# Attention and mixture of experts in one kernel on one Trainium2 core: the last small chunk alone ahead of its pair, three weight units converted ahead, local products in halves

## The chip, the cores and the metric

The kernel runs on one core of one Trainium2 chip, in one launch. The metric is the device time of that launch in microseconds (us). Lower is better.

## What is computed

The reference does two things one after the other. Attention takes q, k, v of 4 batches, 8 heads, 576 tokens and 64 values per head:

```python
q_d = q.reshape(B, H, Sd, factor, D).mean(axis=3)      # factor 4; the same for k and v
out_d = sm_attn(q_d, k_d, v_d)                         # softmax attention over 144 mean tokens
out_up = np.repeat(out_d, factor, axis=2)
mask = np.abs(pos[:, None] - pos[None, :]) < factor    # local: 7 keys for each token
attn = softmax(where(mask, scale * q @ k.T, -1e9))
x = (out_up + attn @ v)                                # as 2304 tokens x 512 values
```

The second part mixes 8 experts over these tokens. The gate P comes from `x @ w_gate` by 8 rounds of normalising rows and columns over all 2304 tokens, so no expert's output can be weighted before all of x is known:

```python
for e in range(E):                                     # 8 experts, D = 512, F = 1024
    h = np.maximum(x @ w1[e], 0.0)
    out += P[:, e:e + 1] * (h @ w2[e])
```

## The kernel before, in words

**Chunks and units.** The 576 mean tokens of the four batches lie behind each other and are cut into six chunks: three small ones (0, 1 and 5, 64 mean tokens, which are 256 tokens) and three large ones (2, 3, 4, 128 mean tokens, 512 tokens). The experts' work is cut into units. A unit is one expert and one eighth of its hidden values for one piece, a piece being a small chunk alone, a pair of small chunks, or a large chunk. `order` (L1001 to L1004) is the list of pieces and experts, eight units each: chunk 0 alone with 4 experts (units 0 to 31, counted from 0), the pair (0, 1) with the other 4 (32 to 63), chunk 2 with 8 (64 to 127), then the pair (1, 5) with 4 and chunk 5 alone with 4 (128 to 191). Chunks 3 and 4 come last in another form (L1401 on, seven products in place of eight).

**One unit on the engines.** `mm1` (L952) multiplies x by a 512 x 128 block of w1 into `psh`, 12 matmuls; ScalarE writes `hh`, the relu rounded to fp32r, and VectorE writes `hl`, what the rounding lost (L970). `mm2` (L975) multiplies these by w2 into `psy`, 3 matmuls for each 128 tokens. TensorE's order is mm1 of unit n+1, then mm2 of unit n, so `hl` of a unit is wanted one mm1 after it can be made. Each raw weight tile `r` becomes a high part (`w1h`, `w2h`, ScalarE, L196) and a low part (`w1l`, `w2l`, GpSimd at L203 or VectorE at L206) in `w_convert` (L185). Three units of raw tiles are held, and four converted units.

**Local attention.** `l_gen` (L268) works through nine local units (one for a small chunk, two for a large one). For each of four heads VectorE multiplies queries by a window of keys (`prod`, L277) and sums (L300); softmax; then it multiplies values by weights (L339) and sums into `lo` (L370). `x_gen` (L757) transposes `lo` on TensorE (`psx`), adds the mean attention (`xs`, L783) and splits x into high (L792) and low (L796 GpSimd, L799 VectorE). Mean attention itself is `d_gen`, fed by sums on GpSimd (`p_gen`, L424: L449 and L453).

**What sets the order.** Instructions of each engine run in the order in which the program writes them. That order is set by a planner with its own clocks (`clk`) and costs: `dma` (L154) for transfers, `pump` (L934) which lets the local thread go ahead between an mm1 and its `hl` as long as the planned VectorE time is 2.5 us short of the planned `hh`. A loop in the first phase (L1130) steps all threads until x of the next piece is there, before it writes the next mm1. When the gate is known the first phase ends at the next full group of eight units; results until then are spilled to DRAM (L1150) and read back (`back_load`, L1207) by the second phase.

In `w_convert` the name `l2` is an argument and later a tile, so that the test on it is always true for the second weight, and GpSimd makes every `w2l`:

```python
    def w_convert(*deps, need=1e9, l2=None):
        ...
        l2 = pl.tile([128, DM], F32R, tag="w2l", name="w2l")
        ...
            if l2 != nc.vector if r is r2 and l2 is not None else t_pool <= max(need, t_dve + 1):
```

Of the kernel before, what the change touches and what calls it, by code (L numbers as in the profile page):

```python
# [20 lines left out]
def attention_moe_kernel(  # L21
# [10 lines left out]
    nc = tc.nc  # L32
    B, H, S, D = q.shape
    NT, DM = out.shape
    E = moe_w_gate.shape[1]
# [118 lines left out]
    def dma(kb, *deps):  # L154

        return at("dma", 0.05 + kb * 0.375, *deps) + 2.0
# [28 lines left out]
    def w_convert(*deps, need=1e9, l2=None):  # L185
# [9 lines left out]
        for r, h, l in ((r1, h1, l1), (r2, h2, l2)):  # L195
            nc.scalar.activation(out=h, in_=r, func=AF.Copy)  # L196
            t = act(512, t_raw, *deps)
            t_pool = max(clk["pool"], t) + 1.3
            if r is r2 and can("p", clk["pool"]):
                t_pool += 1  # L200
            t_dve = max(clk["dve"], t) + 0.6
            if l2 != nc.vector if r is r2 and l2 is not None else t_pool <= max(need, t_dve + 1):
                nc.gpsimd.tensor_tensor(out=l, in0=r, in1=h.bitcast(F32), op=ALU.subtract)  # L203
                done = max(done, pool(512, t))
            else:
                nc.vector.tensor_tensor(out=l, in0=r, in1=h.bitcast(F32), op=ALU.subtract)  # L206
                done = max(done, dve(512, t))
# [60 lines left out]
    def l_gen():  # L268

        for u in range(len(lunits)):  # L270
# [17 lines left out]
            nr = R  # L288
# [4 lines left out]
            for h in range(4):  # L293
                pr, t = ahead[h] if h in ahead else (prod_tile(ap1), 0.0)
                for r0 in range(0, R, nr):
# [7 lines left out]
                    dve(nr * W * D, t)  # L303
            if u + 1 < len(lunits):
                l_load_win(u + 1, k, l_k)
                l_load_q(u + 1)
# [69 lines left out]
            if u + 1 < len(lunits):  # L376
                l_load_win(u + 1, v, l_v)
# [574 lines left out]
    def mm1(piece, n):  # L952
# [16 lines left out]
        pump(t, t_h - 2.5)  # L969
        nc.vector.scalar_tensor_tensor(  # L970
# [21 lines left out]
    with tc.manual_schedule():  # L992
# [11 lines left out]
        order += [((1, NC - 1), e) for e in range(n_small)] + [((NC - 1,), e) for e in range(n_small, E)]  # L1004
# [78 lines left out]
        while not x_ok(0):  # L1083
# [15 lines left out]
            if n_cv[0] < 4 and v_done and max(w_raw[n_cv[0]][2], clk["act"], clk["pool"] - 1.0) <= r:  # L1099
                w_convert()  # L1100
                continue
            th[nm].step()
        while n_cv[0] < 4:
            w_convert(need=0.0)
        started[0] = True
# [17 lines left out]
        while True:  # L1123
# [6 lines left out]
            while n_cv[0] < 4:  # L1130
                w_convert(need=0.0)
# [199 lines left out]
        for si, (piece, e, f, n) in enumerate(steps):  # L1331
# [9 lines left out]
            while n_cv[0] < min(n + 5, len(units)):  # L1341
                w_convert(t2, l2=nc.vector if len(piece) == 1 else nc.gpsimd)
# [3 lines left out]
            if si >= 4:  # L1346
# [4 lines left out]
                next(tg, None)  # L1351
# [206 lines left out]
```

## Time and profile before

| what | value |
|---|---|
| runs | 1683.18, 1675.39, 1684.88 us (median 1683.18) |
| profiled execution, own time | 1685.94 us |
| its span | 1684.2 us |
| TensorE busy | 1645.5 us, 98% of the span |
| VectorE, ScalarE, GpSimd busy | 959.1, 642.5, 997.4 us |
| HBM | 125 GB/s over the span |

The span is the time from the first to the last instruction in the profile. TensorE's matmuls are pipelined: one of 512 columns is shown with 0.39 us, but the next one starts 0.227 us later. So its work is read from starts, and its losses from idle time and from the granted clock. "psy L982 <- DVE hl L970" reads: the matmul of line 982, which writes `psy`, waited for VectorE's instruction of line 970, which writes `hl`.

### The profile page before, as it was taken

To read this page: it belongs to the slowest core of one execution; us is meant where nothing else is said; L and a number is where in the kernel's file an instruction comes from. 1 tells how busy PE (TensorE), PEld (TensorE's weight loads), DVE (VectorE), ACT (ScalarE), POOL (GpSimd) and SP (SyncE) were. 2 spreads that over 40 slices of the span, in tenths; PEclk is the share of its full clock that TensorE was granted. 3 is DMA by queue.
4 is the path that set the end of the run, shared out by engine and by line. 5 is a ranking of instruction groups with operands and counts; after the bars stand their busy time and mean duration, and the time that the engine had idled before them with its cause. 6 is when DMAs were issued, how large, how long until landed. Compare 5 with 4: busy or idle time off the path is not lost.

```text
span 1684.2 us, 22138 instructions
## 1 busy us (share of the span) xinstructions
PE 1645.5 (98%) x7941; PEld 1357.0 (81%) x7941; DVE 959.1 (57%) x1130; ACT 642.5 (38%) x1306; POOL 997.4 (59%) x803
## 2 busy tenths in 40 slices
PE   6899899999999999999999999999999999999999
PEld 5788788788788877887888898888888888888887
DVE  7567896788779677343865324444444444444444
ACT  1554354444444443333333554333333333333332
POOL 5678787669669465444545897554444445444441
PEclk9999999999999999999999999999999999999999
DMA  8877677567577653344665762111111111111111
GB/s 192 188 220 192 167 196 194 160 171 175 170 172 185 155 143 118 107 120 137 197 209 187 229 186 87 53 55 56 51 50 50 51 51 51 53 54 56 50 38 50
DMA packets 220623, 211.70 MB, mean 126 GB/s; under 512 B 12898, under 2 KB 161904, under 8 KB 220514
## 3 DMA queue, kind: packets, MB, share of 16 engines
q1 hardware_dynamic: 211298, 193.51, 42.4%
q10 hardware_dynamic: 9216, 16.78, 2.7%
q8 instruction: 62, 1.02, 0.3%
q14 instruction: 47, 0.39, 0.1%
HBM read 190.85 MB, written 19.40 MB: 125 GB/s over the span
## 4 chain that ended last, share of the span: by engine, by line
PE 86%; POOL 5%; DMA 4%; DVE 3%; issue 2%; ACT 1%; SPq 0%; POOLq 0%; ACTq 0%; DVEq 0%
PE psh L961 22%; PE psm L1401 18%; PE psy L980 7%; PE psy L982 7%; PE psy L981 7%; PE psy L1474 7%; PE psy L1472 7%; PE psy L1473 7%; POOL w2l L203 2%; POOL w1l L203 2%; DMA r<-in_moe_w_dram 1%; DVE lo L370 1%; DMA lq<-in_q_dram 1%; DMA dr<-in_v_dram 1%; PE pss L674 1%
## 5 line engine op out<-in xcount | busy, mean ns | idle before, releaser
L203 POOL TENSOR_TENSOR w1l<-r,w1h 128x512 fp32r<-128x512 f32 x191 | 264.5, 1385 | 233.8 <-ACT w1h L196 205.8
L203 POOL TENSOR_TENSOR w2l<-r,w2h 128x512 fp32r<-128x512 f32 x192 | 289.7, 1509 | 73.0 <-ACT w2h L196 72.8
L980 PE MATMUL psy<-w2h,hh 128*128 128x512 f32 x640 | 255.6, 399 | 3.6 <-ACT hh L967 3.6
L982 PE MATMUL psy<-w2h,hl 128*128 128x512 f32 x640 | 250.8, 392 | 7.7 <-DVE hl L970 6.4
L970 DVE SCALAR_TENSOR_TENSOR hl<-psh,hh 128x512 fp32r<-128x512 f32 (+1 forms) x192 | 114.9, 599 | 244.0 <-ACT hh L967 243.5
L981 PE MATMUL psy<-w2l,hh 128*128 128x512 f32 x640 | 250.6, 392 | 0.0
L1319 POOL TENSOR_TENSOR w2l<-r,w2h 128x512 fp32r<-128x512 f32 x64 | 83.2, 1300 | 281.3 <-ACT w2h L1318 281.3
L1195 DVE SCALAR_TENSOR_TENSOR acc<-psy,lg,acc 128x512 f32<-128x512 f32 x140 | 103.9, 750 | 199.9 <-PE psy L1474 198.7
L967 ACT ACTIVATE hh<-psh 128x512 fp32r<-128x512 f32 (+1 forms) x192 | 100.7, 525 | 300.3 <-PE psh L961 297.8
L196 ACT ACTIVATE w2h<-r 128x512 fp32r<-128x512 f32 x192 | 120.9, 630 | 195.7 <-POOL w1l L203 103.3
L961 PE MATMUL psh<-xhs,w1h 128*128 128x256 f32 (+1 forms) x512 | 177.4, 346 | 0.6 <-ACT xhs L792 0.6
L961 PE MATMUL psh<-xls,w1h 128*128 128x256 f32 (+1 forms) x512 | 174.9, 342 | 0.5 <-POOL xls L796 0.4
L961 PE MATMUL psh<-xhs,w1l 128*128 128x256 f32 (+1 forms) x512 | 174.5, 341 | 0.0
L1285 POOL TENSOR_TENSOR c1l<-r,c1h 128x512 fp32r<-128x512 f32 (+1 forms) x128 | 145.0, 1159 | 33.9 <-ACT c1h L1282 33.9
L982 PEld LDWEIGHTS psy<-w2h,hl 128*128 128x128 f32 x640 | 120.5, 188 | 35.9 <-DVE hl L970 8.3
L980 PEld LDWEIGHTS psy<-w2h,hh 128*128 128x128 f32 x640 | 121.0, 189 | 26.2 <-ACT hh L967 3.8
L981 PEld LDWEIGHTS psy<-w2l,hh 128*128 128x128 f32 x640 | 121.0, 189 | 21.7
L1282 ACT ACTIVATE c1h<-r 128x512 fp32r<-128x512 f32 (+1 forms) x128 | 65.0, 567 | 176.0 <-POOL r L1290 176.0
L196 ACT ACTIVATE w1h<-r 128x512 fp32r<-128x512 f32 x192 | 120.0, 625 | 25.0 <-DMA r<-in_moe_w_dram 15.4
L370 DVE TENSOR_REDUCE lo<-prod 128x256 f32<-128x1792 f32 x36 | 123.5, 3433 | 8.3 <-PE psx L774 8.1
L961 PEld LDWEIGHTS psh<-xhs,w1h 128*128 128x128 f32 x512 | 98.8, 193 | 13.9 <-ACT xhs L792 1.4
L961 PEld LDWEIGHTS psh<-xls,w1h 128*128 128x128 f32 x512 | 99.1, 194 | 13.1 <-POOL xls L796 0.7
(183 smaller groups left out, 3568.4 us busy)
## 6 DMA issues: line engine op xcount, KB each, us to landing
r<-in_moe_w_dram SPq DMA_DIRECT2D x512, 256.0 KB
spill<-sp ACTq DMA_DIRECT2D x56, 256.0 KB
s<-spill SPq DMA_DIRECT2D x56, 256.0 KB
dr<-in_k_dram SPq DMA_DIRECT2D x32, 144.0 KB
dr<-in_v_dram SPq DMA_DIRECT2D x32, 144.0 KB
dr<-in_q_dram SPq DMA_DIRECT2D x24, 144.0 KB
lw<-in_v_dram SPq DMA_DIRECT2D x4, 640.0 KB
lw<-in_k_dram SPq DMA_DIRECT2D x2, 1120.0 KB
```

What stands on the lines that cost most here:

```text
L196: nc.scalar.activation(out=h, in_=r, func=AF.Copy)
L203: nc.gpsimd.tensor_tensor(out=l, in0=r, in1=h.bitcast(F32), op=ALU.subtract)
L370: nc.vector.tensor_reduce(out=ot[:, r0:r0 + nr, h % 2], in_=pr[:, r0:r0 + nr].rearrange("p r w d -> p r d w"), axis=AX.X, op=ALU.add,)
L961: nc.tensor.matmul(out=ps, lhsT=w[:, kk], rhs=x[:, kk], start=(i == 0), stop=(i == len(seq) - 1))
L980: nc.tensor.matmul(out=y, lhsT=hh[:, ts], rhs=h2, start=(f == 0), stop=False)
L981: nc.tensor.matmul(out=y, lhsT=hh[:, ts], rhs=l2, start=False, stop=False)
L982: nc.tensor.matmul(out=y, lhsT=hl[:, ts], rhs=h2, start=False, stop=(f == NF - 1))
L1285: nc.gpsimd.tensor_tensor(out=ls[i][:, s], in0=r[:, s], in1=hs[i][:, s].bitcast(F32), op=ALU.subtract)
L1401: nc.tensor.matmul(out=ps, lhsT=wt[:, kk], rhs=xt[:, kk], start=start and j == 0, stop=j == len(seq) - 1, skip_group_check=not start,)
L1472: nc.tensor.matmul(out=y, lhsT=hh[:, f, ts], rhs=h2, start=(f == 0), stop=False)
L1473: nc.tensor.matmul(out=y, lhsT=hh[:, f, ts], rhs=l2, start=False, stop=False)
L1474: nc.tensor.matmul(out=y, lhsT=hl[:, f, ts], rhs=h2, start=False, stop=(f == 3))
```

## The change

Six edits, most of them to the planner. (1) The planner's cost of a transfer goes from 0.375 to 0.55 us per unit of size. (2) `w_convert` gets an argument `low2` of its own name; VectorE makes `w2l` for units of a chunk alone in the second phase. (3) Local products and sums are issued in halves of two tokens of the four, from local unit 1 on; the load of the value window of local unit 1 moves from the end of local unit 0 to a place inside local unit 1. (4) Three units are converted before the first mm1, not four, and the planner's clocks are set to their maximum there; after each of the first two mm1 the local thread is stepped until 1.5 us of VectorE time have passed. (5) Chunk 5 alone comes ahead of the pair (1, 5). (6) Spilled tiles are read back during the pair alone, and the preparation of the last phase takes one step per unit.

```diff
-        return at("dma", 0.05 + kb * 0.375, *deps) + 2.0
+        return at("dma", 0.05 + kb * 0.55, *deps) + 2.0
-    def w_convert(*deps, need=1e9, l2=None):
+    def w_convert(*deps, need=1e9, low2=nc.gpsimd):
-            if l2 != nc.vector if r is r2 and l2 is not None else t_pool <= max(need, t_dve + 1):
+            if low2 is nc.gpsimd if r is r2 else t_pool <= max(need, t_dve + 1):
...
-            nr = R
+            nr = R if u == 0 else R // 2
...
+                if u == 1 and h == 0:
+
+                    l_load_win(1, v, l_v)
...
-            if u + 1 < len(lunits):
+            if 0 < u < len(lunits) - 1:
                 l_load_win(u + 1, v, l_v)
...
         pump(t, t_h - 2.5)
+        if n < 2:
+
+            was = clk["dve"]
+            while clk["dve"] < was + 1.5:
+                th["l"].step()
...
-        order += [((1, NC - 1), e) for e in range(n_small)] + [((NC - 1,), e) for e in range(n_small, E)]
+        order += [((NC - 1,), e) for e in range(n_small, E)] + [((1, NC - 1), e) for e in range(n_small)]
...
-            if n_cv[0] < 4 and v_done and max(w_raw[n_cv[0]][2], clk["act"], clk["pool"] - 1.0) <= r:
+            if n_cv[0] < 3 and (v_done or n_cv[0] < 2) and max(w_raw[n_cv[0]][2], clk["act"], clk["pool"] - 1.0) <= r:
...
-        while n_cv[0] < 4:
+        while n_cv[0] < 3:
             w_convert(need=0.0)
+        now = max(clk["dve"], clk["act"], clk["pool"])
+        clk["pe"] = clk["dve"] = clk["act"] = now
...
-            while n_cv[0] < 4:
-                w_convert(need=0.0)
...
-                w_convert(t2, l2=nc.vector if len(piece) == 1 else nc.gpsimd)
+
+                alone = len(steps[n_cv[0] - n_a][0]) == 1
+                w_convert(t2, low2=nc.vector if alone else nc.gpsimd)
...
-            if si >= 4:
+            if len(piece) == 2:
+
                 for _ in range(2):
                     back_load()
                     back_load()
                     back_add()
-                next(tg, None)
+            if si >= 4:
                 next(tg, None)
```

Because a planner writes the order, the diff doesn't tell where instructions end up. Three places matter. In the changed kernel lines are numbered up to 11 higher from L304 on.

ScalarE at the start, where x of chunk 0 is made (`xhs`) and the first two units begin (`hh`). The raw tile of the fourth unit is r_419 before and r_413 in the change. Before:

```order
L196 ACTIVATE w1h<-r_173 128x512
L196 ACTIVATE w2h<-r_174 128x512
L792 ACTIVATE xhs<-xs 128x256 x4
L196 ACTIVATE w1h<-r_419 128x512
L196 ACTIVATE w2h<-r_420 128x512
L967 ACTIVATE hh<-psh 128x256 x2
L819 ACTIVATE gs<-psg 16x256
```

and now:

```order
L196 ACTIVATE w1h<-r_173 128x512
L196 ACTIVATE w2h<-r_174 128x512
L603 ACTIVATE od<-pso 128x2x64 x2
L795 ACTIVATE xhs<-xs 128x256 x4
L970 ACTIVATE hh<-psh 128x256 x2
L822 ACTIVATE gs<-psg 16x256
L196 ACTIVATE w1h<-r_413 128x512
L196 ACTIVATE w2h<-r_414 128x512
```

The fourth unit's conversion now stands behind the two `hh`, where it stood ahead of them.

VectorE at the last local unit (chunk 5), the value products and sums up to the last `xs`. Before, in units 108 to 114:

```order
L339 TENSOR_TENSOR prod<-lw,sc 128x1792
L970 SCALAR_TENSOR_TENSOR hl<-psh,hh 128x512
L370 TENSOR_REDUCE lo<-prod 128x4x64
L339 TENSOR_TENSOR prod<-lw,sc 128x1792
L970 SCALAR_TENSOR_TENSOR hl<-psh,hh 128x512
L370 TENSOR_REDUCE lo<-prod 128x4x64
L339 TENSOR_TENSOR prod<-lw,sc 128x1792
L970 SCALAR_TENSOR_TENSOR hl<-psh,hh 128x512
L783 TENSOR_TENSOR xs<-psx,od 128x256
```

and now, from `hl` of unit 127 (first row here) to `hl` of units 128 to 130 (last row); the first rows and the last:

```order
L978 SCALAR_TENSOR_TENSOR hl<-psh,hh 128x512
L342 TENSOR_TENSOR prod<-lw,sc 128x896
L373 TENSOR_REDUCE lo<-prod 128x2x64
L342 TENSOR_TENSOR prod<-lw,sc 128x896
L373 TENSOR_REDUCE lo<-prod 128x2x64
...
L342 TENSOR_TENSOR prod<-lw,sc 128x896
L373 TENSOR_REDUCE lo<-prod 128x2x64
L786 TENSOR_TENSOR xs<-psx,od 128x256 x2
L978 SCALAR_TENSOR_TENSOR hl<-psh,hh 128x256 x3
```

Between those two `hl` there stand 6 products, 6 sums and 4 `xs`; before, no two `hl` of this stretch have more than one product and one sum between them, and the last `xs` of chunk 5 stands ahead of `hl` of unit 114.

TensorE at the same place of the change: the end of mm2 of unit 126, the transposes of chunk 5's `lo`, and mm1 of unit 128.

```order
L990 MATMUL psy<-w2h,hl 128x512
L777 MATMUL psx<-ident,lo 128x64 x16
L964 MATMUL psh<-xhs,w1h 128x256
L964 MATMUL psh<-xls,w1h 128x256
L964 MATMUL psh<-xhs,w1l 128x256
```

mm2 of unit 127 stands behind this mm1. Before, these transposes stand at units 111 and 114, and the first phase ends at unit 128; now it ends at unit 152, with 62 spilled tiles in place of 56.

## Rows read from the trace of the kernel before

**Rows 1.** The page's part 1, busy time of each engine.

```profile
PE 1645.5 (98%) x7941; PEld 1357.0 (81%) x7941; DVE 959.1 (57%) x1130; ACT 642.5 (38%) x1306; POOL 997.4 (59%) x803
```

**Rows 2.** Busy time by stretch: from:to, length, then busy us (and instructions) of PE, PEld, DVE, ACT, POOL, the granted clock, DMA share, GB/s.

```profile
0.00:60.00 60.00, 42.29 (x288) 32.20 (x288) 38.66 (x52) 13.99 (x41) 32.28 (x24) 1.00 0.94 197
60.00:180.00 120.00, 106.46 (x708) 92.68 (x709) 86.79 (x85) 60.62 (x145) 98.04 (x71) 0.94 0.70 196
180.00:760.00 580.00, 578.08 (x2748) 470.47 (x2747) 420.14 (x411) 251.32 (x545) 384.33 (x268) 1.00 0.59 159
760.00:1050.00 290.00, 288.32 (x1444) 244.26 (x1444) 138.70 (x187) 118.12 (x217) 185.92 (x146) 1.00 0.58 178
1050.00:1684.00 634.00, 630.37 (x2758) 517.43 (x2756) 274.84 (x397) 198.44 (x358) 296.82 (x295) 1.00 0.17 51
```

**Rows 3.** TensorE's timeline (start, us, instruction, in brackets the idle time before it and what ended it): the end of mm1 of unit 1 and mm2 of unit 0, the four later waits of the first 180 us, and two rows of an undisturbed unit, 11 matmuls apart.

```profile
57.17 0.28 PE L961 MATMUL psh<-xhs,w1h 128*128 128x256 f32 x1
...
58.48 0.28 PE L961 MATMUL psh<-xhs,w1l 128*128 128x256 f32 x1
62.35 0.50 PE L980 MATMUL psy<-w2h,hh 128*128 128x512 f32 x1 [3.58 <-ACT hh L967]
...
112.18 0.50 PE L982 MATMUL psy<-w2h,hl 128*128 128x512 f32 x1 [1.26 <-DVE st L692]
...
118.78 0.48 PE L705 MATMUL pst<-ident,pp 80*72 80x80 f32 x2 [2.41 <-ACT pp L685]
...
151.41 0.43 PE L774 MATMUL psx<-ident,lo 64*128 64x64 f32 x4 [2.14 <-DVE lo L370]
...
176.19 0.59 PE L982 MATMUL psy<-w2h,hl 128*128 128x512 f32 x1 [4.79 <-DVE hl L970]
...
191.09 0.39 PE L980 MATMUL psy<-w2h,hh 128*128 128x512 f32 x1
...
193.58 0.39 PE L982 MATMUL psy<-w2h,hl 128*128 128x512 f32 x1
```

**Rows 4.** ScalarE's timeline at the start.

```profile
60.70 0.63 ACT L196 ACTIVATE w1h<-r 128x512 fp32r<-128x512 f32 x1 [7.09 <-DMA r<-in_moe_w_dram]
...
61.93 0.64 ACT L967 ACTIVATE hh<-psh 128x256 fp32r<-128x256 f32 x2
```

**Rows 5.** The clock: stretches of 3.4 us that follow the waits which ended at 62.35, 118.78, 151.41 and 176.19 us, with the columns of rows 2.

```profile
63.80:67.20 3.40, 3.40 (x16) 3.09 (x15) 2.15 (x2) 1.19 (x3) 3.40 (x3) 0.50 0.52 153
118.40:121.80 3.40, 3.02 (x15) 3.02 (x16) 2.65 (x4) 2.54 (x7) 1.58 (x3) 0.50 0.83 260
152.60:156.00 3.40, 3.40 (x15) 2.85 (x14) 1.09 (x3) 1.21 (x3) 0.68 (x2) 0.50 0.94 160
176.50:179.90 3.40, 3.40 (x9) 2.65 (x8) 3.40 (x3) 0.00 (x0) 1.16 (x2) 0.50 0.22 74
```

**Rows 6.** GpSimd and VectorE at the same times: GpSimd's start after the first wait; a VectorE product at 166.08 us with the `hl` behind it, and GpSimd's instructions meanwhile; then `hl` of unit 31.

```profile
61.41 1.27 POOL L203 TENSOR_TENSOR w1l<-r,w1h 128x512 fp32r<-128x512 f32 x1 [7.10 <-DMA r<-in_moe_w_dram]
...
166.08 9.71 DVE L277 TENSOR_TENSOR prod<-lq,lw 128x1792 f32<-128x1792 f32 x1
175.72 0.41 DVE L970 SCALAR_TENSOR_TENSOR hl<-psh,hh 128x256 fp32r<-128x256 f32 x1
...
166.43 1.29 POOL L203 TENSOR_TENSOR w1l<-r,w1h 128x512 fp32r<-128x512 f32 x1
...
172.64 1.27 POOL L203 TENSOR_TENSOR w2l<-r,w2h 128x512 fp32r<-128x512 f32 x1
173.86 3.06 POOL L449 TENSOR_TENSOR dr<-dr 72x512 f32<-72x512 f32 x1
...
102.80 1.27 POOL L449 TENSOR_TENSOR dr<-dr 72x512 f32<-72x512 f32 x1
...
177.01 0.73 POOL L453 TENSOR_TENSOR dq<-dr 72x256 f32<-72x256 f32 x1
...
177.98 0.41 DVE L970 SCALAR_TENSOR_TENSOR hl<-psh,hh 128x256 fp32r<-128x256 f32 x1
178.31 2.01 DVE L277 TENSOR_TENSOR prod<-lq,lw 128x1792 f32<-128x1792 f32 x1
```

**Rows 7.** Groups of instructions by line and shape: busy us, mean ns of one, idle before and its releasers. The row of xl has 512 elements and two SBUF operands.

```profile
L370 DVE TENSOR_REDUCE lo<-prod 128x256 f32<-128x1792 f32 x36 | 123.5, 3433 | 8.3 <-PE psx L774 8.1
...
L277 DVE TENSOR_TENSOR prod<-lq,lw 128x1792 f32<-128x1792 f32 x34 | 94.2, 2772 | 3.6 <-DMA lw<-in_k_dram 3.0
...
L970 DVE SCALAR_TENSOR_TENSOR hl<-psh,hh 128x512 fp32r<-128x512 f32 x128 | 88.0, 687 | 147.0 <-ACT hh L967 146.7
...
L1410 DVE SCALAR_TENSOR_TENSOR xl<-cc,xh 128x512 fp32r<-128x512 f32 x64 | 45.0, 703 | 45.4 <-ACT xh L1407 45.4
...
L967 ACT ACTIVATE hh<-psh 128x512 fp32r<-128x512 f32 x128 | 76.4, 597 | 248.6 <-PE psh L961 246.6 <-DVE tmp L871 2.0
```

**Rows 8.** Four rows of the start, which give the pieces of making x of a small chunk: the transposes on TensorE, `xs` and the last low part on VectorE, a low part on GpSimd.

```profile
48.77 1.17 PE L774 MATMUL psx<-ident,lo 64*128 64x64 f32 x16
...
49.57 0.42 DVE L783 TENSOR_TENSOR xs<-psx,od 128x256 f32<-128x256 f32 x1 [4.14 <-PE psx L774]
...
53.64 0.95 DVE L799 TENSOR_TENSOR xls<-xs,xhs 128x256 fp32r<-128x256 f32 x1 [0.48 <-ACT xhs L792]
...
53.59 0.72 POOL L796 TENSOR_TENSOR xls<-xs,xhs 128x256 fp32r<-128x256 f32 x1
```

## The prediction, as it was put on record before the change ran

> **What bounds the kernel now.** I read the page's part 1 first: TensorE is busy 98% of the span [rows 1]. Both kernels issue the same matmuls, so what a change can win is TensorE's idle time and its slow stretches, and nothing else. The table by stretch says where these lie [rows 2]: 17.7 us are idle in the first 60 us, 13.5 in the 120 after, then 1.9 in 580, 1.7 in 290 and 3.6 in 634. From 180 us on there is next to nothing to win, and everything to lose: a wait of TensorE placed there counts in full.
>
> The timeline of TensorE names the waits [rows 3]. mm2 of unit 0 begins 3.58 us late for `hh`. Four later ones (1.26, 2.41, 2.14 and 4.79 us) are waits for VectorE's work, the second by way of ScalarE. Those over 2 us are followed by 3.4 us at a granted clock of 0.50, which is 1.2 in place of 2.4 GHz, and each such stretch costs 1.7 us [rows 5].
>
> Two rows per engine show what stands behind. `hh` at 61.93 us was queued on ScalarE behind the conversion of the fourth unit, which had waited 7.09 us for its raw tile [rows 4]. And the `hl` at 175.72 us was queued behind a local product that shows 9.71 us, where one alone takes 2.01 [rows 6]. GpSimd ran six weight subtractions back to back meanwhile, from 166.43 to 173.9 us, and the next GpSimd instruction shows 3.06 us, as the product got its turn. So products with two SBUF operands and GpSimd's subtractions exclude each other here, and the product lost several times in a row.
>
> On this last point the Trainium skill (SBUF — State Buffer, section "SBUF: two separate sides") says that VectorE and GpSimd share a port pair as an exclusive lock, and that whichever starts first holds it for its whole instruction. By that a product would wait for one subtraction at most, 1.3 us, and the row shows 7.7. The row decides, and halving doubles how often VectorE must ask.
>
> **The change part by part.** I number units from 0.
>
> *Start.* The fourth unit's conversion now stands behind both `hh` on ScalarE. The 3.58 us go, and with them the slow stretch behind: -5.3 us at the start of mm2 of unit 0. VectorE has two half products and two half sums ahead of the first two `hl`. The x parts are through VectorE at 54.6 us in the trace [rows 8]; a half product and a half sum, 1.09 us each (below), put `hl` of unit 0 at 57.2, while TensorE is at mm1 of unit 1 until 58.6 [rows 3]. That is hidden. The fourth unit's conversion comes after `hh` of unit 1, so GpSimd, which stood idle until 61.41 [rows 6], goes on at about 59.5.
>
> *Units 2 to 31.* A small unit alone costs TensorE 12 matmuls of 256 columns at (58.48 - 57.17)/11 = 0.12 us and 6 of 512 at (193.58 - 191.09)/11 = 0.227 us: 2.8 us [rows 3]. GpSimd's two subtractions take 2.56 us of it and exclude the products. So I count what the port pair has to do up to `hl` of unit 31. Before, by the program's order: 58 subtractions at 1.28, three sums each of 1.27 and 0.73, ten products at 2.01, and 2 us of small parts make 102 us. From 61.4 that is 164, and the product ahead of unit 30 ended at 175.8: 12 us were lost on top. Now: 56 subtractions (71.7), seven sums of each kind, since the planner puts eight more of them here (14.0), 21 half products at 1.09 (22.9), three subtractions on VectorE at 0.70 and 2.5 of small parts: 113 us, from 59.5 to 172.5. Against `hl` of unit 31, which ended at 178.4, the gain is 6 us at best, and if the 12 us are lost again it is 6 us of loss. New long stretches speak for some loss: three products and three sums now stand ahead of `hl` of unit 18 (8.9 us against a unit of 2.8), and 5.9 us ahead of unit 30. Halves mean shorter waits elsewhere. I take -4 for the start and this stage together, between -6 and +6.
>
> *Price of a half.* A subtraction of 512 elements with two SBUF operands takes 0.70 us, a product of 1792 takes 2.01 [rows 6, 7]; on that line 896 cost 0.70 + 384 x 1.31/1280 = 1.09. A half sum of L300 is put at the same. The value sum of L370 takes 3.43 [rows 7], half of it and 0.04 is 1.75. In all 128 instructions are added, some 20 us of VectorE, which is busy 57% of the span [rows 1].
>
> *Units 32 to 127.* Only 1.9 us of idle time are left there. Halves and the planner's margin may take 1 of it: -1, between -2 and +3 (twice as many requests to the port pair).
>
> *Unit 128.* Chunk 5 alone now follows chunk 2, so its x is wanted at unit 128. In the change's order VectorE has, behind `hl` of unit 127, six half products, six half sums and four `xs`; TensorE has behind mm2 of unit 126 the transposes of these sums, then mm1 of unit 128, and only then mm2 of unit 127. Nothing on TensorE can go past. Let T be the end of mm1 of unit 127. `hh` and `hl` take 0.60 and 0.69 [rows 7] and some 0.15 of passing on: T + 1.45. Then 6 x 1.09 + 6 x 1.75 + 4 x 0.42 = 18.7 [rows 8]: T + 20.1. ScalarE's high part (0.4, as an `hh` of that size [rows 4]) and GpSimd's low part (0.72) of the last quarter, with two steps of 0.1, give T + 21.4, and a quarter of mm1 is then left, 0.4. Undisturbed, TensorE would be through with mm2 (2.7), transposes (1.2) and mm1 (1.4) at T + 5.3. So the end moves by 16.5 us. The slow stretch that followed each wait over 2 us adds 1.7 [rows 5]: **+18.2**. Low: halves at exactly half, 2.7 for a pair, and no slow stretch, 15. High: each product waits once for a subtraction, 6 x 1.3 more, 26. The value taken stands near the low end, since GpSimd soon runs out of free weight tiles while TensorE waits.
>
> *The rest.* The gate falls into small units alone (129 to 151), whose VectorE pieces are 2.3 us against 2.8. The six more spills are on engines with slack. `w2l` on VectorE is three instructions. The last phase now starts from a pair, 5.4 us a unit, with more time for its conversions: -0.5, between -1 and +2. The read-back is as dense as before.
>
> Sum: -4 - 1 + 18.2 - 0.5 = +12.7. The profiled execution took 1685.94 us, 2.8 above the median of the runs shown, which is the figure to meet; 1683.2 + 12.7 = **1696 us**.
>
> **The rivals.** *Not slower:* all waits of the first 180 us vanish but the loads that nothing hides. Then 3.6 at the start, 11.2 of later waits (13.5 less the 2.3 of the first that fall behind 60 us [rows 2, 3]) and four slow stretches (6.8) make -21.6 in place of -4, and the sum is -5: 1678. It decides if units 2 to 31 run at 3.1 us each. For it: halves let `hl` in sooner. Against it: 113 us of work for one port pair. *Products wait twice as often:* the mean product waits 2.77 - 2.01 = 0.75 us now [rows 7]; with twice as many requests 26 half products in units 2 to 31 wait 20 us together. Half of that on the path, and the high end at unit 128, makes it 8 more: 1704. By the Trainium skill's rule (SBUF — State Buffer, section as above), at most one subtraction of 1.3 us for each request, 26 requests would wait 33 us at most, and the time would be near this one too. *The wait at 128 is not there:* the sums of chunk 5 are done earlier than the order says; then -5.5, 1678 as well. The order of one engine leaves no room for it, unless TensorE itself is late.
>
> **How the numbers follow.** Forecast 0.60, 1689 to 1702 for itself. Waits twice as often 0.17. No waits in the first stage 0.16. No wait at unit 128 0.07. 0.5% of 1683 is 8.4 us, about what can be told from no change: slower begins at 1691.6, faster at 1674.8. Of the forecast 0.85 lies above 1691.6, with the second case 0.68; faster is a third of the two last cases and less, 0.05; 0.27 are left for no change. The range for all, 1679 to 1706, takes in part of the two cases below.
>
> **What would show it.** In the changed profile: no wait of TensorE for `hh` near 58 us and no conversion ahead of it on ScalarE; `hl` of unit 31 between 172 and 184 us; one gap of 14 to 20 us on TensorE near 750 us, put down to the parts of x of chunk 5 (`xls`, `xhs`), with VectorE busy through all of it and a stretch at clock 0.50 behind it. I am wrong if that gap is under 8 us, or if `hl` of unit 31 comes before 168 us.

## The result: 1.0086 times the time before, and the profile after

The changed kernel takes 1696.85 us (median of 5 runs, 1695.82 to 1699.23), the kernel before 1681.19 beside it (5 runs): ratio 1.0086, 95% interval 1.0056 to 1.0115, so some 14 us slower. The profiled execution took 1696.62 us, 10.7 more than that of before. The forecast was 1696.

Part 1 of the page, which answers to [rows 1], has 61 us more of VectorE and nothing more of TensorE:

```profile
PE 1643.2 (97%) x7941; PEld 1355.7 (80%) x7941; DVE 1020.1 (60%) x1266; ACT 641.3 (38%) x1312; POOL 962.8 (57%) x795
```

The table by stretch of the changed kernel, with the columns of [rows 2] (TensorE busy first, the granted clock third from the end); the last three rows cut the stretch from 180 us on closer:

```profile
0.00:60.00 60.00, 44.02 (x347) 34.45 (x348) 47.53 (x62) 18.47 (x51) 37.42 (x29) 0.72 0.94 206
60.00:180.00 120.00, 107.25 (x689) 92.42 (x690) 92.67 (x104) 59.74 (x153) 102.25 (x76) 0.96 0.76 200
180.00:760.00 580.00, 563.84 (x2668) 460.50 (x2668) 428.47 (x443) 241.74 (x521) 345.12 (x256) 0.99 0.58 155
760.00:1050.00 290.00, 287.59 (x1440) 242.79 (x1439) 172.26 (x255) 119.91 (x226) 175.26 (x134) 1.00 0.62 191
1050.00:1684.00 634.00, 634.00 (x2775) 520.49 (x2775) 276.97 (x400) 201.43 (x364) 302.74 (x301) 1.00 0.17 50
...
180.00:700.00 520.00, 519.15 (x2465) 423.95 (x2465) 383.47 (x402) 225.86 (x491) 320.60 (x236) 1.00 0.62 164
700.00:800.00 100.00, 84.11 (x452) 71.74 (x451) 67.34 (x93) 36.76 (x74) 53.70 (x43) 0.91 0.40 121
800.00:1050.00 250.00, 248.17 (x1192) 207.60 (x1191) 149.92 (x205) 99.03 (x182) 146.08 (x112) 1.00 0.62 192
```

The reader is to see one row: from 700 to 800 us TensorE is idle for 15.9 us, at a mean clock of 0.91. In the kernel before, the same stretch shows 98.85 us busy at 1.00:

```profile
700.00:800.00 100.00, 98.85 (x442) 81.34 (x441) 39.76 (x85) 35.42 (x61) 45.48 (x36) 1.00 0.43 130
```

The idle times of the other stretches up to 1050 us are within 1.8 us of before, three of the four better. The clock of the first row, 0.72 against 1.00 in [rows 2], is no such gap between the kernels as far as their matmuls show it: the gate's products of 256 columns (`psg`) start 0.21 us apart in both (55.59, 55.81 and 56.02 us before, 51.15, 51.36 and 51.57 now), against 0.12 at the full clock [rows 3], though the profile of before gives 1.00 there. Behind 1050 us nothing is lost: the 3.6 us that [rows 2] shows idle there lie in the last 14 us of the kernel before, and the last 14 of this one, outside the row, have 4.3.

TensorE's waits by what ended them (total, times, longest):

```profile
PE psx L777 <- DVE lo L373: 17.1, 5, 8.2
...
PE psh L964 <- POOL w1l L203: 6.6, 8, 2.4
PE psh L964 <- ACT w1h L196: 3.5, 2, 3.1
...
PE psy L990 <- DVE hl L978: 2.1, 3, 1.2
```

15.3 of the 17.1 us lie at unit 128; the fifth wait, 1.78 us, ends at 144.35 us. TensorE's timeline at unit 128 has four waits of the transposes (`psx`) for VectorE's `lo`:

```profile
739.20 0.34 PE L777 MATMUL psx<-ident,lo 64*128 64x64 f32 x2 [2.54 <-DVE lo L373]
...
741.91 0.70 PE L777 MATMUL psx<-ident,lo 64*128 64x64 f32 x6 [2.37 <-DVE lo L373]
...
750.83 0.44 PE L777 MATMUL psx<-ident,lo 64*128 64x64 f32 x2 [8.22 <-DVE lo L373]
...
753.45 0.69 PE L777 MATMUL psx<-ident,lo 64*128 64x64 f32 x6 [2.18 <-DVE lo L373]
```

VectorE's timeline of the same 18 us: six half products, six half sums and `xs` between `hl` of unit 127 and the last quarter of x. The only pause is 0.64 us, ahead of the last two `xs`.

```profile
734.62 0.69 DVE L978 SCALAR_TENSOR_TENSOR hl<-psh,hh 128x512 fp32r<-128x512 f32 x1 [0.74 <-ACT hh L970]
735.23 2.19 DVE L342 TENSOR_TENSOR prod<-lw,sc 128x896 f32<-128x896 f32 x1
737.45 1.70 DVE L373 TENSOR_REDUCE lo<-prod 128x128 f32<-128x896 f32 x1
739.07 1.07 DVE L342 TENSOR_TENSOR prod<-lw,sc 128x896 f32<-128x896 f32 x1
...
751.71 1.68 DVE L373 TENSOR_REDUCE lo<-prod 128x128 f32<-128x896 f32 x1
754.03 0.76 DVE L786 TENSOR_TENSOR xs<-psx,od 128x256 f32<-128x256 f32 x2 [0.64 <-PE psx L777]
757.76 0.42 DVE L978 SCALAR_TENSOR_TENSOR hl<-psh,hh 128x256 fp32r<-128x256 f32 x1 [2.97 <-ACT hh L970]
```

The table by stretch for VectorE's 18 us, and for the one slow stretch of the clock around them:

```profile
735.23:753.40 18.17, 2.91 (x17) 1.85 (x15) 17.95 (x15) 1.46 (x3) 4.28 (x4) 0.68 0.12 34
741.86:758.93 17.07, 6.62 (x35) 5.47 (x36) 12.57 (x13) 1.97 (x5) 3.19 (x4) 0.50 0.00 0
```

VectorE is busy for 17.95 of 18.17 us. The clock fell to 0.50, which is 1.2 of 2.4 GHz, at 741.86 us, inside the waits, and stayed there for 17.07 us; TensorE's 6.62 us of work in it cost some 3.3 us more than at full clock. After 758.93 us it is at 1.00 to the end of the work.

The start, which answers to [rows 4, 6]: ScalarE's first `hh`, then the fourth unit's conversion behind the second; GpSimd's first subtraction of that unit; TensorE's first two instructions of mm1 of unit 0; and the `hl` of unit 31 on VectorE.

```profile
51.02 0.38 ACT L970 ACTIVATE hh<-psh 128x256 fp32r<-128x256 f32 x1 [2.06 <-PE psh L964]
54.10 0.39 ACT L970 ACTIVATE hh<-psh 128x256 fp32r<-128x256 f32 x1 [2.70 <-PE psh L964]
...
54.65 0.61 ACT L196 ACTIVATE w1h<-r 128x512 fp32r<-128x512 f32 x1
...
55.34 2.00 POOL L203 TENSOR_TENSOR w1l<-r,w1h 128x512 fp32r<-128x512 f32 x1 [5.91 <-ACT w1h L196]
...
46.03 0.39 PE L964 MATMUL psh<-xhs,w1h 128*128 128x256 f32 x1 [0.60 <-ACT xhs L795]
48.48 0.39 PE L964 MATMUL psh<-xls,w1h 128*128 128x256 f32 x1 [2.06 <-POOL xls L799]
...
172.70 0.41 DVE L978 SCALAR_TENSOR_TENSOR hl<-psh,hh 128x256 fp32r<-128x256 f32 x1
```

`hh` of units 0 and 1 stood together at 61.93 us before; they are at 51.02 and 54.10 now. GpSimd goes on at 55.34 in place of 61.41, and `hl` of unit 31 ends at 173.1 in place of 178.4 us.

### The profile page after: what moved, and what is told of

It reads as the page before. It is cut to its first block, busy times and chain, and to the rows that moved or that the text cites. A ratio compares the mean times of both kernels' runs of the same rounds, so it can differ in the third digit from the quotient of the medians.

```text
span 1694.8 us, 22262 instructions
## 1 busy us (share of the span) xinstructions
PE 1643.2 (97%) x7941; PEld 1355.7 (80%) x7941; DVE 1020.1 (60%) x1266; ACT 641.3 (38%) x1312; POOL 962.8 (57%) x795
## 4 chain that ended last, share of the span: by engine, by line
PE 89%; DMA 3%; DVE 3%; POOL 2%; issue 2%; ACT 1%; SPq 0%; ACTq 0%; POOLq 0%; DVEq 0%
PE psh L964 24%; PE psm L1412 18%; PE psy L988 8%; PE psy L990 8%; PE psy L989 8%; PE psy L1485 7%; PE psy L1483 7%; PE psy L1484 7%; POOL w2l L203 1%; POOL w1l L203 1%; DVE lo L373 1%; DVE prod L342 1%; PE psv L524 1%; DMA dr<-in_v_dram 1%; DMA r<-in_moe_w_dram 1%
## 5 line engine op out<-in xcount | busy, mean ns | idle before, releaser
L203 POOL TENSOR_TENSOR w1l<-r,w1h 128x512 fp32r<-128x512 f32 x186 | 257.4, 1385 | 260.1 <-ACT w1h L196 247.8
L203 POOL TENSOR_TENSOR w2l<-r,w2h 128x512 fp32r<-128x512 f32 x187 | 270.0, 1445 | 74.6 <-ACT w2h L196 73.4
L1327 POOL TENSOR_TENSOR w2l<-r,w2h 128x512 fp32r<-128x512 f32 x64 | 83.2, 1299 | 284.1 <-ACT w2h L1326 284.1
L373 DVE TENSOR_REDUCE lo<-prod 128x128 f32<-128x896 f32 (+1 forms) x68 | 127.8, 1881 | 1.4
L964 PEld LDWEIGHTS psh<-xhs,w1l 128*128 128x128 f32 x512 | 98.8, 193 | 18.7 <-POOL w1l L203 8.5
```

The source lines that it names most:

```text
L373: nc.vector.tensor_reduce(out=ot[:, r0:r0 + nr, h % 2], in_=pr[:, r0:r0 + nr].rearrange("p r w d -> p r d w"), axis=AX.X, op=ALU.add,)
L964: nc.tensor.matmul(out=ps, lhsT=w[:, kk], rhs=x[:, kk], start=(i == 0), stop=(i == len(seq) - 1))
```

## The experiments

The theory after the result, called A below: the 14 us are the wait at unit 128 alone. It comes from the halves and not from the order of the units, since either order wants x of chunk 5 at unit 128. The planner starts a local step ahead of an `hl` whenever VectorE's planned time is 2.5 us short of `hh`, however long the step is. Of a pair's or large chunk's 5.4 us that leaves 5.4 - 0.69 - 2.5 = 2.2 us in which steps may start: a whole product of 2.01 and then still a whole sum of 3.43, 5.4 us together, but of half steps two or three, 2.2 to 3.9 us. (These are measured lengths. The planner counts 1.94 us for every whole step and 1.00 for every half, so that two whole ones or three halves start.) In the order of the instructions the transposes of chunk 5 move accordingly from units 111 to 114 to unit 128, and the gate's last sums from unit 126 to unit 149. Rivals: the order makes the wait (B); the halves cost everywhere, by more turns at the port that VectorE and GpSimd share (C).

**1. Halves alone** (on the kernel before):

```diff
-            nr = R
+            nr = R if u == 0 else R // 2
```

> The kernel before with one edit alone: local products and sums in halves from the second chunk on; order of the units, start and prices of the planner as before. Theory A (the whole loss is the wait at unit 128, and it comes from the halves: they leave chunk 5's local work so late that its transposes stand at unit 128): the wait shows here too, 15 to 20 us of idle TensorE near 750 us before psx, and the time is the kernel before plus 14 to 20, so 1695 to 1701 us. Theory B (the wait comes from chunk 5 alone standing first in the order after chunk 2): no idle time over 4 us near 750 us, and 1679 to 1686 us. Theory C (the halves cost everywhere, by twice as many turns at the port that VectorE and GpSimd share): hl of unit 31 later than 178.4 us and idle time spread over 180 to 740 us, 1688 to 1695 us.

Measured: ratio 1.0309 (1.0279 to 1.0340), 1736.8 us. The wait at unit 128 is there, in the old order: gaps of 5.43, 2.24, 8.23 and 2.18 us. B is out. But some 52 us were lost, not 14 to 20. Two losses were not foreseen: 14.4 us of the same wait for `lo` near 170 us (chunk 1's x, wanted at unit 32), and thirteen waits for `hl` of 21.8 us in all, from 905 us on.

**2. Whole again** (on the changed kernel):

```diff
-            nr = R if u == 0 else R // 2
+            nr = R
```

> The changed kernel with products and sums whole again, all else as changed. Theory A: chunk 5's transposes come some 20 units before unit 128, no idle time over 4 us between 700 and 800 us, and the changed kernel less 17 to 20: 1676 to 1680 us, if the start keeps its gain (hl of unit 31 at 170 to 178 us). Theory B (the order is what makes the wait): 10 us or more idle near 750 us still, 1690 to 1698 us. Theory C (halves gain at the start by shorter waits for the port): hl of unit 31 at 178 us or later, 1680 to 1686 us even if the wait at unit 128 goes.

Measured: 1.0001 (0.9983 to 1.0018), 1684.5 us, as C had it. The wait at unit 128 is gone, as A had it. The table by stretch shows what came in its place:

```profile
60.00:180.00 120.00, 103.26 (x689) 87.69 (x689) 98.54 (x103) 58.91 (x156) 102.88 (x72) 0.96 0.77 208
...
700.00:800.00 100.00, 100.00 (x533) 86.48 (x532) 44.93 (x77) 45.83 (x85) 37.49 (x30) 1.00 0.45 143
```

From 700 to 800 us TensorE is never idle; from 60 to 180 it is idle for 16.7 us, against 12.75 with halves, and `hl` of unit 31 ends at 183.2 us, 10 later than with halves. So the halves gain in the units of chunk 0 and lose later.

**3. A smaller margin** (on the changed kernel):

```diff
-        pump(t, t_h - 2.5)
+        pump(t, t_h - 1.5)
```

> The changed kernel with its halves, but the planner may put a local step ahead of an hl if it ends up to 1.5 in place of 2.5 us before the hh. Theory A (halves are late because the planner lets too few of them in): chunk 5's transposes stand 11 units or more before unit 128, no idle time over 4 us near 750 us, small waits for hl grow by at most 3 us in all; 1677 to 1682 us. Theory B (order): 10 us or more idle near 750 us, 1690 to 1698 us. Theory C (the halves themselves cost): the wait at 128 shrinks, but idle time in 60 to 740 us grows by 8 us or more, 1687 to 1697 us.

Measured: 1.0048 (1.0033 to 1.0063), 1693.3 us. The wait at unit 128 is gone, which bears out the arithmetic of the margin, but the time is C's. TensorE's waits say where it went:

```profile
PE psy L990 <- DVE hl L978: 11.1, 7, 2.8
...
PE psx L777 <- DVE xs L786: 6.4, 4, 2.2
```

Waits for `hl` grow from 2.1 to 11.1 us, and 6.4 us of waits for `xs` are new; from 180 to 700 us TensorE is busy 507.5 us of 520, where it was 519.15. What the margin lets in stands ahead of an `hl`. How much it lets in can be read between `hl` of unit 31 and `hl` of unit 63: products and their sums take VectorE 139 us here, 95 in the changed kernel, and 116 with whole ones (experiment 2).

**4. The old order** (on the changed kernel; its rules of the last phase kept):

```diff
-        order += [((NC - 1,), e) for e in range(n_small, E)] + [((1, NC - 1), e) for e in range(n_small)]
+        order += [((1, NC - 1), e) for e in range(n_small)] + [((NC - 1,), e) for e in range(n_small, E)]
```

> The changed kernel with the pair of chunks 1 and 5 ahead of chunk 5 alone again, as before the change; halves and start as changed. Theory A: either order wants x of chunk 5 at unit 128, so the wait stays: 12 to 20 us idle near 750 us, 1692 to 1700 us. Theory B: no wait over 4 us near 750 us, 1676 to 1682 us.

Measured: 1.0322 (1.0295 to 1.0350), 1739.8 us: neither. The wait at unit 128 stays (2.54, 2.37, 8.22 and 2.17 us), so A is right on that and B wrong; but a second wait came, in this kernel's waits and in its table by stretch:

```profile
PE psm L1412 <- ACT cs L1439: 40.8, 1, 40.8
...
1033.00:1074.00 41.00, 1.02 (x5) 0.48 (x3) 24.41 (x30) 0.00 (x0) 5.80 (x6) 0.56 0.73 225
```

VectorE adds 30 spilled results in these 41 us, with 16.5 us of waits for them to come back. The rule that reads spills back beside pairs only finds few pairs behind the gate in the old order.

**5. Halves in one chunk** (on the changed kernel; the second local chunk is the one worked off in units 2 to 31):

```diff
-            nr = R if u == 0 else R // 2
+            nr = R // 2 if u == 1 else R
```

> The changed kernel with halves in the second local chunk only (the one that is worked off in units 2 to 31), whole products and sums in the later ones. Theory A (halves help where the units are small and wait for the shared port, and cost where a pair's window of planning lets one step through): start and units 2 to 31 as in the changed kernel (hl of unit 31 within 2 us of 173.1), no idle time over 4 us near 750 us, the gate shut by unit 128: the kernel before less 1 to 8 us, ratio 0.995 to 0.999. Theory C (whole products in the later chunks give the gain back by waits for the port in units 32 to 110): idle time and slow stretches between 180 and 700 us 6 us or more above the changed kernel's 11.7; ratio 1.000 to 1.005.

Measured: 0.9971 (0.9947 to 0.9995), 1679.9 us. A holds in every point: `hl` of unit 31 at 173.4 us, 99.31 us busy from 700 to 800. It is the only version here whose interval lies below the kernel before, and the halves in the later chunks cost 1.0086 - 0.9971 = 1.15%, 19 us.

**6. Halves in the scores only** (on the changed kernel; ahead of the value loop):

```diff
+            nr = R
             t_sc = clk["dve"]
```

> The changed kernel with halves for the scores only; value products and value sums whole. Theory A (the steps of half a value sum, 1.75 us, are what delays chunk 5: of them and of half products fewer microseconds fit ahead of an hl under the 2.5 us rule): chunk 5's transposes come 13 units or more before unit 128 and no idle time over 4 us stands near 750 us; ratio to the kernel before 0.994 to 1.001. Theory D (any halves delay it on the chip): 8 us or more idle near 750 us, ratio 1.004 to 1.010.

Measured: 0.9993 (0.9969 to 1.0017), 1682.5 us; from 700 to 800 us TensorE is busy for 99.31 us. A. Halved scores alone do not delay chunk 5; it takes the halved value steps as well (these alone were not tried).

**7. The old start** (on the changed kernel; halves and order kept):

```diff
-                if u == 1 and h == 0:
-                    l_load_win(1, v, l_v)
...
-            if 0 < u < len(lunits) - 1:
+            if u + 1 < len(lunits):
...
-        if n < 2:
-            was = clk["dve"]
-            while clk["dve"] < was + 1.5:
-                th["l"].step()
...
-            if n_cv[0] < 3 and (v_done or n_cv[0] < 2) and max(...) <= r:
+            if n_cv[0] < 4 and v_done and max(...) <= r:
...
-        while n_cv[0] < 3:
+        while n_cv[0] < 4:
             w_convert(need=0.0)
-        now = max(clk["dve"], clk["act"], clk["pool"])
-        clk["pe"] = clk["dve"] = clk["act"] = now
```

> The changed kernel with the start of the kernel before: four units converted ahead, nothing of the local work forced ahead of the first two hl, its value window loaded at the end of a chunk. Halves and order as changed. Theory A (the start's gain is real and is what the table by stretch shows): the wait for hh near 58 us and a slow stretch behind it are back, hl of unit 0 about 10 us later than in the changed kernel; and VectorE has some 8 us more to do at unit 128, so the wait there is 20 to 30 us in place of 17: the changed kernel plus 10 to 18 us, ratio to the kernel before 1.014 to 1.020. Theory E (a later start is made good in units 2 to 31, where the port sets the pace): hl of unit 31 within 3 us of 173.1 and ratio 1.007 to 1.012.

Measured: 1.0184 (1.0135 to 1.0232), 1715.1 us. A: the wait for `hh` is back (3.55 us), `hl` of unit 0 ends at 60.8 in place of 52.75 us, that of unit 31 at 181.1 in place of 173.1, and the waits at unit 128 are 11.2, 2.2, 8.2 and 2.2 us, 24 together. What is late at the start stays late through units 2 to 31.

**8. The old order with its own rules** (experiment 4, and):

```diff
-                alone = len(steps[n_cv[0] - n_a][0]) == 1
-                w_convert(t2, low2=nc.vector if alone else nc.gpsimd)
+                w_convert(t2, low2=nc.vector if len(piece) == 1 else nc.gpsimd)
...
-            if len(piece) == 2:
+            if si >= 4:
                 for _ in range(2):
                     back_load()
                     back_load()
                     back_add()
-            if si >= 4:
+                next(tg, None)
                 next(tg, None)
```

> The pair of chunks 1 and 5 ahead of chunk 5 alone again, and with it the rules of the last phase as before: spills read back in every step from the fourth, w2l on VectorE by the step that runs and not by the unit that is converted. Halves and start as changed. The earlier run with the old order alone had one gap of 40.8 us at 1033.6 us, behind the sums that read the spills. Theory F (that gap belongs to the rule that reads spills back beside pairs only, and not to the order): no gap over 10 us near 1034 us; what is left over the changed kernel is the waits for hl of 1.1 to 3.4 us that the run with halves alone shows from 943 to 1045 us, 20 to 30 us: ratio to the kernel before 1.018 to 1.028. Theory G (too few pairs are left after the gate in the old order, whatever the rule): a gap of 25 us or more, ratio over 1.03.

Measured: 1.0244 (1.0197 to 1.0292), 1725.9 us: F. The gap of 41 us is gone, and so belonged to the rule. What is left over the changed kernel is 1.6% or 27 us. Some 21 of them are idle time of TensorE from 800 to 1050 us (22.5 us, 1.8 in the changed kernel); the others were not placed. This kernel's waits and its VectorE show the cause:

```profile
PE psy L990 <- DVE hl L978: 23.5, 22, 3.0
...
1014.24 0.75 DVE L1203 SCALAR_TENSOR_TENSOR acc<-s,lg,acc 128x512 f32<-128x512 f32 x1 [2.02 <-DMA s<-spill]
1015.57 1.10 DVE L1203 SCALAR_TENSOR_TENSOR acc<-s,lg,acc 128x512 f32<-128x512 f32 x1 [0.57 <-DMA s<-spill]
1016.59 0.41 DVE L978 SCALAR_TENSOR_TENSOR hl<-psh,hh 128x256 fp32r<-128x256 f32 x1
```

An `hl` stands behind a sum that waits 2.02 us for a spill. From 943 to 1045 us TensorE is busy 80.6 us here and 101.2 in the changed kernel. The reason is argued from the lengths of the units: since halves let the gate shut late, the old order has mainly chunk 5 alone left, 2.8 us a unit, to read all spills back beside, and the new order leaves pairs of 5.4 us for it.

**9. The order alone** (experiment 7's old start, and whole products):

```diff
-            nr = R if u == 0 else R // 2
+            nr = R
```

> The changed kernel with whole products and sums and with the start of the kernel before: what is left of the change is the new order of the units with its rules of the last phase and the dearer transfers of the planner. Theory A (the order is worth nothing as long as the gate shuts before unit 128, as it does here and in the kernel before): no idle time over 4 us from 700 us on, ratio to the kernel before 0.998 to 1.003. Theory H (the order gains by itself, as a last phase that begins with pairs has more time for its conversions): at least 4 us less idle time from 700 us on, ratio 0.993 to 0.997.

Measured: 1.0049 (1.0026 to 1.0072), 1692.9 us: neither. A is right on the place: TensorE is never idle from 700 to 1050 us, where it was for 1.8 us before, and the last 14 us are as before (3.8 us idle), so the order gains 2 us of idle time at most and not H's 4. But `hl` of unit 31 ends at 190.2 us, 11.8 later than before. Up to that unit this kernel differs from the one before only in the planner's price of a transfer (0.55 for 0.375). VectorE's value sums from 60 to 190 us, of before and then of this kernel:

```profile
L370 DVE TENSOR_REDUCE lo<-prod 128x256 f32<-128x1792 f32 x4 | 13.7, 3426 | 0.0
```

```profile
L370 DVE TENSOR_REDUCE lo<-prod 128x256 f32<-128x1792 f32 x7 | 23.7, 3385 | 0.1
```

Three whole sums more, and three products with them, were put where the units are shortest.

Experiments 1 and 7 are a second pair that differs up to unit 31 in this price alone, here with halves. `hl` of unit 31 ends at 169.4 us with the old price and at 181.1 with the new one. But with the old price x of chunk 1 comes too late, which is the 14.4 us of experiment 1, and `hl` of unit 33 ends at 195.1 and 194.1 us: what the dearer price delays here is made good two units later.

**10. Experiment 5 with the old start** (both diffs above):

> The run with halves in the second local chunk only, with the start of the kernel before. Theory A (the start is worth what the first 60 us show, 3.6 us of wait and 1.7 of slow clock): ratio to the kernel before 1.000 to 1.003, so 5 to 9 us above the same kernel with the new start. Theory E (units 2 to 31 are paced by GpSimd and the shared port, and make a late start good): hl of unit 31 within 3 us of 173.4 and ratio 0.996 to 0.999.

Measured: 1.0034 (1.0012 to 1.0056), 1688.1 us; `hl` of unit 31 at 179.0 us. The start is worth 0.63%, 11 us, a little over A's range; E is out.

**11. Halves in twos** (on the changed kernel, for the scores and alike for the values):

```diff
                 for r0 in range(0, R, nr):
-                    if h not in ahead:
+                    if h not in ahead and r0 == 0:
                         yield tk[h]
-                        qk_prod(h, nc.vector, pr, r0, nr)
-                    yield t
+                        for r1 in range(0, R, nr):
+                            qk_prod(h, nc.vector, pr, r1, nr)
+                    if r0 == 0:
+                        yield t
```

> The changed kernel with all its halves, but the planner takes both half products of a head as one step and both half sums as one step, with no look at the margin between them. Theory A (what delays chunk 5 is how many steps the planner lets in, not how many instructions VectorE issues): chunk 5's transposes stand 9 to 14 units ahead of unit 128, no idle time over 4 us near 750 us; ratio to the kernel before 0.997 to 1.003. Theory C (twice as many instructions wait twice as often for the shared port, and that is the cost): 8 us or more of the loss stays, spread over 180 to 740 us, ratio 1.005 to 1.010.

Measured: 1.0070 (1.0049 to 1.0092), 1694.1 us. A is right on the wait (99.2 us busy from 700 to 800), C on the time. The two are different losses: the steps decide when chunk 5 is ready, and long steps in units 2 to 31 cost what they cost with whole instructions (`hl` of unit 31 at 185.9 us). Another 5.8 us are idle from 180 to 700 us. VectorE at 100 us shows one such pair of steps between two `hl`:

```profile
100.13 0.44 DVE L982 SCALAR_TENSOR_TENSOR hl<-psh,hh 128x256 fp32r<-128x256 f32 x1
100.46 3.68 DVE L344 TENSOR_TENSOR prod<-lw,sc 128x896 f32<-128x896 f32 x2
104.07 3.30 DVE L377 TENSOR_REDUCE lo<-prod 128x128 f32<-128x896 f32 x2
107.29 0.41 DVE L982 SCALAR_TENSOR_TENSOR hl<-psh,hh 128x256 fp32r<-128x256 f32 x1
```

7.2 us lie between two `hl` of units of 2.8 us, and behind the second stands a weight's low part (`w1l`) that the planner gave to VectorE; TensorE waits 6.29 us for it, up to 108.35 us. (The profile puts this wait down to `st`, which is cleared at 108.25 us, just behind this low part.)

**12. 24 units of chunk 0 alone** (on experiment 5):

```diff
-        n_small = 4
+        n_small = 3
```

> The run with halves in the second local chunk only, with 24 in place of 32 units of the first small chunk alone at the start, so that the stretch whose pace GpSimd's subtractions set is 8 units shorter. Theory I (that stretch loses by its pace): idle time and slow stretches of 60 to 180 us fall from 28 to 20 us or less, ratio to the kernel before 0.991 to 0.996. Theory J (the second chunk's x, wanted at unit 24 now, is late): one wait of 5 us or more near 140 us, behind some 12 us of VectorE work, ratio 0.999 to 1.006.

Measured: 1.0106 (1.0067 to 1.0146), 1700.9 us. J's wait came (5.68 us for `lo` at 145.6 us, 1.39 and 1.90 behind it), I's gain did not (103.7 us busy from 60 to 180, 3.7 less than in experiment 5). The time is above both ranges, by a wait nobody had named: 16.1 us of `psm` for `cs` from 1017.9 us on, the wait of experiment 4. The likely reason, not tried apart, is that three pairs in place of four are left for the spills.

## Why the prediction was right

The time came out in the range, and by the forecast's own case: a wait at unit 128 of the size forecast. What the wait was put down to is wrong, and the first term is right by luck. Against the terms of the sum:

- *Start and units 2 to 31*, -4: `hl` of unit 31 ends 5.3 us earlier. The two halves of the term were mis-sized against each other. The start gained more: `hl` of unit 0 ends 10.0 us earlier and not 5.5 (57.2 was forecast for it), as the prediction took x of chunk 0 to be through VectorE when it was before [rows 8], while the first matmul of unit 0 now starts at 46.03 us, 4.5 earlier. Units 2 to 31 gave 4.7 of it back: 117.8 us from GpSimd's restart at 55.34 to `hl` of unit 31, where 113 were counted for the port. That the two errors nearly cancel is luck.
- *Price of a half*: 1.07 to 1.09 us for a product that waits for nothing, as forecast, and 1.68 to 1.70 for a value sum (1.75). The groups of the changed kernel, which answer to [rows 7], give the price with its waits:

```profile
L373 DVE TENSOR_REDUCE lo<-prod 128x128 f32<-128x896 f32 x64 | 114.7, 1792 | 1.4
L342 DVE TENSOR_TENSOR prod<-lw,sc 128x896 f32<-128x896 f32 x64 | 98.6, 1540 | 0.5
L277 DVE TENSOR_TENSOR prod<-lq,lw 128x896 f32<-128x896 f32 x64 | 98.4, 1538 | 0.9 <-DMA lq<-in_q_dram 0.5
```

  A half product waits (1.54 - 1.08) = 0.46 us, 128 of them 59 us; the 67 whole ones waited 34 x 0.76 + 33 x 0.59 = 45 us. So the rival *products wait twice as often* had the sign, at 1.3 times in place of 2. It is not what moved the end. VectorE's work grew by 61 us in all, where the prediction counted some 20 for the halves: products and sums show 34 more with their waits, and 17 are low parts of weights that the planner gave to VectorE (11 instructions, one before).
- *Units 32 to 127*, -1: from 180 to 700 us TensorE is idle for 0.85 us, before 1.83. Right.
- *Unit 128*, +18.2: from 700 to 800 us TensorE is idle 15.9 - 1.15 = 14.7 us longer, and 3.3 us go to the slow clock, 18.0 together; the sum had 16.5 and 1.7. VectorE is busy for 18.7 us between `hl` of unit 127 and of unit 128, as the sum had it. But the prediction put the wait down to `xls` and `xhs` and to one gap: it is four gaps, the longest 8.2 us, ended by `lo`, as the transposes wait for the half sums. And it gave a wrong cause. "Chunk 5 alone now follows chunk 2, so its x is wanted at unit 128" is true of the old order as well, and experiments 1, 4 and 8 have the wait in that order. The halves make it: experiments 2, 5 and 6 take them away, wholly or in part, and lose it, each with the new order. Experiments 3 and 11 keep all halves, let the planner start more of them, and lose it too.
- *The rest*, -0.5: TensorE is idle 1.2 us longer from 800 to 1050 us, and 0.5 in the last 14. That is +1.7, of the other sign than forecast, though inside the term's range (up to +2). Hidden in it is what the new order saves, 27 us which the late gate would else have cost, most of them waits behind sums that read spills (experiment 8).

These parts come to -5.3 - 1 + 18 + 1.7 = +13.4 us, between the profiled execution's +10.7 and the 14 us of the ratio. The rival *not slower* failed because waits in the first 180 us did not vanish (28.7 us idle there, 31.3 before). *No wait at 128* is what experiments 5 and 6 show.

Taken apart by ratios, the change is four things: order, rules and the planner's price +0.5% (experiment 9), the start -0.5% on top of it (experiment 2), halves in the second chunk -0.3% (5, whose interval touches that of 2), halves in all later ones +1.15%. These shares hold for this order of taking apart: the start is worth 0.6% with halves in one chunk (experiment 10) and 1.0% with all of them (experiment 7). What stays open: that the price of 0.55 delays `hl` of unit 31 by 12 us rests on two pairs of kernels which up to there differ in nothing else, but what it does to the whole time was not tried alone, nor was experiment 5 with the old price.

## What to carry to other kernels

A planner that may start a step of any length inside a margin gets less done when the steps are halved (95 in place of 116 us of local work over 32 units here); look at when the last of the work lands, not only at how long a step holds up the queue. Cut steps fine where the units beside them are short (here 2.8 us) and leave them whole where they are long (5.4 us) and the work has a due time. The first half of this advice is worth 0.3% here, from two runs whose intervals touch; the second is worth 1.15%. And an edit that looks idle in the sum may be what keeps another one cheap: the new order shows next to no gain without the halves and, with its rules, 27 us with them.

## What the runs showed of the hardware

A half product can lose to GpSimd's instructions several times in a row too. VectorE and GpSimd of the changed kernel at 138 us:

```profile
138.07 4.24 DVE L342 TENSOR_TENSOR prod<-lw,sc 128x896 f32<-128x896 f32 x1
...
136.86 1.30 POOL L203 TENSOR_TENSOR w2l<-r,w2h 128x512 fp32r<-128x512 f32 x1
138.12 0.74 POOL L456 TENSOR_TENSOR dv<-dr 72x256 f32<-72x256 f32 x1
138.81 1.29 POOL L203 TENSOR_TENSOR w1l<-r,w1h 128x512 fp32r<-128x512 f32 x1
140.06 1.30 POOL L203 TENSOR_TENSOR w2l<-r,w2h 128x512 fp32r<-128x512 f32 x1
142.94 1.27 POOL L203 TENSOR_TENSOR w1l<-r,w1h 128x512 fp32r<-128x512 f32 x1 [1.58 <-ACT w1h L196]
```

It shows 4.24 us where one alone takes 1.08. Three instructions of GpSimd run from end to end meanwhile, the last until 141.36 us. The product ends at 142.31, 0.95 us later, while GpSimd waits for ScalarE. The Trainium skill (SBUF — State Buffer, section "SBUF: two separate sides") has whichever of the two engines starts first hold the shared pair of ports for its whole instruction. By an estimate from this rule and the rows, the product would wait 0.1 us for the subtraction that runs as it begins and ends at 138.16, or 0.8 us if the next instruction goes ahead of it too; the rows show 3.2.

The clock's slow stretch at the waits of 736 to 753 us was 17.07 us long, where those behind the single waits of before were 3.4 [rows 5]. It began inside the waits and ended 5.5 us after the last. A single long wait gave the same length: in experiment 12, with 16.1 us of wait up to 1034.03 us, the clock is at 0.50 from 1022.74 to 1039.81 us, with 5.8 us of TensorE's work in it, which cost some 2.9 us; the four waits cost 3.3.
